# Two chunks to an attention block in a sliding-window attention and SwiGLU kernel

## The chip, the cores and the metric

The kernel runs on one core of a Trainium2 chip. A core has a matrix engine (TensorE, PE in the profile, whose weight loads are listed as PEld), three engines for elementwise work (VectorE or DVE, ScalarE or ACT, GpSimd or POOL), a queue engine (SyncE or SP) and 16 DMA engines that move data between the memory of the chip (DRAM) and the core's working memory (SBUF). Matmul results land in PSUM, a small memory of eight banks. The engines run side by side and meet at semaphores.

The metric is the device time of one execution in microseconds (us). Lower is better.

## The reference

Causal attention with a window of 64 positions, then a feed-forward block with a gate. Cut to what is computed:

```python
B, H, S, D = 8, 8, 576, 64
scores = (1 / sqrt(D)) * q @ k.transpose(0, 1, 3, 2)
rel = pos[:, None] - pos[None, :]
scores = where((rel >= 0) & (rel < 64), scores, -1e9)
attn = softmax(scores)
x = (attn @ v).transpose(0, 2, 1, 3).reshape(4608, 512)
g = x @ w_gate                       # 512 -> 1536
silu = g / (1 + exp(-g))
out = (silu * (x @ w_val)) @ w_out   # 1536 -> 512
```

## The kernel before

**Tiles.** The 4608 tokens are 36 chunks of 128 for attention (`NCH`) and nine groups of 512 for the feed-forward part (`NFC`). A sequence of 576 tokens is nine blocks of 64, so a chunk of 128 may hold the end of one sequence and the start of the next; `var` picks one of three masks for that. A token needs the keys of its own block of 64 and of the block ahead of it only.

**Order.** Every operation is recorded once, in program order, with the buffers that it reads and writes (`_Graph.op`, line 42). `emit` (line 63) gives each engine its operations in that order and puts in the semaphore waits that the buffers ask for. A read after a write on TensorE itself needs no wait; the `after=` of an operation asks for one. At the end SyncE waits for the last transfer of every DMA lane (lines 139 to 142).

**Attention of chunk n.** `load` (line 279) brings q, k and v by GpSimd's DMA queue. `T` (line 321) transposes k and q by DMA on SyncE's queue into `kT` and `qT`. `Sb` (line 350) makes the scores on TensorE, in matmuls that use a quarter of the array (64x64): per pair of heads, the first 64 keys of chunk n against all 128 queries (line 391, 64x128), and, in the lower half of the partitions, the block of 64 ahead of the chunk against the first 64 queries and the chunk's second 64 keys against the second 64 queries (line 395, 64x64 each). ACT takes the exponential into `pt` (line 403), and `Sm` (line 407) multiplies by the mask on DVE. `AVmm` (line 426) multiplies by v, 16 matmuls of 64x65 in each of two phases; phase 1 is recorded with `after=` phase 0. The 65th column is the sum of the exponentials, and `AVn` (line 478) divides by it on DVE (lines 484 and 487). `X` (line 506) transposes the result into `xT` by DMA on SyncE's queue.

`B(n)` (line 496) is one attention block: phase 0 of AV for chunk n, the scores of chunk n+1, phase 1 of AV for chunk n, the division, the mask of chunk n+1.

**Feed-forward of group c.** `F(c, fs)` (line 565) makes one of twelve slices of the hidden layer: four matmuls of 512 columns with `Wg`, four with `Wv` (line 585), a tanh on ACT (line 591) and two products on DVE (lines 593 and 595) into `hT`. `O(c, u)` (line 601) is one output tile of 128 tokens: twelve matmuls of 512 columns (line 611), a copy out of PSUM on ACT (line 616) and a store on ACT's queue (line 618). `O_last` (line 620) makes the last tile in two halves of 256 columns (line 633), evicted by ACT and by DVE.

**The loop.** Groups 0 and 1 are written out by hand, with the first chunks among them. From group 2 on a loop runs (lines 814 to 829): each step u of a group c has the block B(4c+u+4), two F, the output tile O(c-1, u) and one F. So group c's steps carry the attention of group c+1. Blocks end with chunk 35, in group 7; group 8 has none.

**PSUM banks.** `bank` (line 215) hands out four banks in turn to F and O, and four to attention.

Of the kernel before, what the change touches and what calls it, by code (L numbers as in the profile page):

```python
# [4 lines left out]
ACTF = mybir.ActivationFunctionType  # L5
# [16 lines left out]
class _Op:  # L22
    __slots__ = ("i", "eng", "fn", "deps", "dma", "pos", "lane", "occ", "clock", "inc", "count")

    def __init__(self, i, eng, fn, deps, dma):
        self.i, self.eng, self.fn, self.deps, self.dma = i, eng, fn, deps, dma
        self.inc = False
        self.count = 0


class _Graph:
# [31 lines left out]
    def emit(self):  # L63
# [59 lines left out]
        def run(eng, e):  # L123
# [15 lines left out]
            if e == "sp":  # L139
                for lane, o in lanes.items():  # L140
                    k, v = target(o)
                    eng.wait_ge(sem[k], v)
# [9 lines left out]
class _Kernel:  # L152
    NQ = 6
    NV = 10
    NZ = 8
    NP = 4
# [4 lines left out]
    NST = 4  # L161

# [6 lines left out]
    def alloc(self):  # L169
# [10 lines left out]
        self.nmask = sb("nmask", 3 * 128)  # L180
        self.Wg = sb("Wg", NK * DFF)[:, :].rearrange("p (c f) -> p c f", c=NK)
# [31 lines left out]
        self.n_s = 0  # L213

    def bank(self, kind):
# [59 lines left out]
    def init_nmask(self):  # L275
        self.g.op("dve", lambda e: e.tensor_scalar(
            self.nmask[:, :], self.mask[:, :], 1.0, 30000.0, ALU.subtract, ALU.mult), reads=["mask"], writes=["nmask"])

# [78 lines left out]
    def Sa(self, n, bias=False):  # L357
        st = [n, [self.bank("a"), self.bank("a")], False]
        if bias:
            self.Sbias(st)  # L360
        return st
# [15 lines left out]
    def Sb(self, st, mask=True):  # L377
# [23 lines left out]
        for p in range(2):  # L401
            po = pt[:, p::2, :]
            g.op("act", lambda e, po=po, p=p: e.activation(po, sv[p], ACTF.Exp, scale=SCALE), reads=[bx[p][1]], writes=[pk[p]])  # L403
        if not bias and mask:
            self.Sm(n)

    def Sm(self, n):
# [3 lines left out]
        m = self.mask[:, 128 * v:128 * v + 128].unsqueeze(1).to_broadcast([128, H, 128])  # L411
        self.g.op("dve", lambda e: e.tensor_tensor(pt, pt, m, ALU.mult), reads=pk + ["mask"], writes=pk)  # L412
# [5 lines left out]
    def AVa(self, n):  # L418
        bx = [self.bank("a"), self.bank("a")]
# [58 lines left out]
    def AVn(self, st):  # L478
# [9 lines left out]
             reads=bk + [("rc", ir)], writes=[("xb", ix, 0), ("xb", ix, 1)])  # L488

# [6 lines left out]
    def B(self, n):  # L496
# [6 lines left out]
        if n + 1 < NCH:  # L503
            self.Sm(n + 1)

# [28 lines left out]
    def first_T(self, engs):  # L534
        g = self.g
        d = self.ck.rearrange("p j h d -> p h j d")
        self.copy("dve", d, self.fk, [("f", 0), ("f", 1)] + self.fkk, [("ost", 0)])
        for c in range(2):
# [8 lines left out]
            g.op("pe", pe, reads=["ident", ("ost", 0)], writes=[bk])  # L547
# [53 lines left out]
    def O(self, c, u):  # L601
        g = self.g
        ih = c % self.NH
        hT = self.hT[ih]
        io = (4 * c + u) % self.NO
        ost = self.ost[io]
        OB, ok = self.bank("f")

        def pe(e):
            for f in range(NF):  # L610
                r = e.matmul(OB[:, :], hT[:, f, 128 * u:128 * u + 128], self.Wo[:, f, :],  # L611
# [4 lines left out]
        g.op("act", lambda e: e.activation(ost[:, :], OB[:, :], ACTF.Copy), reads=[ok], writes=[("ost", io)])  # L616
        r0 = 512 * c + 128 * u
        g.op("act", lambda e: e.dma_start(self.out[r0:r0 + 128, :], ost[:, :]), reads=[("ost", io)], dma=True)

    def O_last(self, c, u):  # L620
        g = self.g
        ih = c % self.NH
        hT = self.hT[ih]
        ost = self.ost[(4 * c + u) % self.NO]
        io = (4 * c + u) % self.NO
        r0 = 512 * c + 128 * u
        for w, eng in ((0, "act"), (1, "dve")):
            OB, ok = self.bank("f")
            cs = slice(256 * w, 256 * w + 256)

            def pe(e, OB=OB, cs=cs):
                for f in range(NF):
                    r = e.matmul(OB[:, 0:256], hT[:, f, 128 * u:128 * u + 128], self.Wo[:, f, cs],  # L633
                                 start=(f == 0), stop=(f == NF - 1))
                return r

            g.op("pe", pe, reads=self.hTk(ih) + [("Wo", f) for f in range(NF)], writes=[ok])
            d, a = ost[:, cs], OB[:, 0:256]
            if eng == "act":
                g.op("act", lambda e, d=d, a=a: e.activation(d, a, ACTF.Copy), reads=[ok], writes=[("ost", io), ("osth", w)])  # L640
            else:
                g.op("dve", lambda e, d=d, a=a: e.tensor_copy(d, a), reads=[ok, ("ost", io)], writes=[("osth", w)])
            q = "sp" if w == 0 else "act"
            g.op(q, lambda e, d=d, cs=cs: e.dma_start(self.out[r0:r0 + 128, cs], d), reads=[("osth", w)], dma=True)
# [56 lines left out]
    def build(self):  # L701
# [174 lines left out]
```

## Time and profile before

| | us |
|---|---|
| three runs | 335.21, 335.66, 335.78 |
| median | 335.66 |
| the profiled execution: its span | 333.5 |
| TensorE's matmuls, busy | 325.2 |
| DVE, busy | 200.8 |
| ACT, busy | 138.5 |
| GpSimd, busy | 107.1 |
| line 585, 512 columns: 768 matmuls, mean | 0.38 |
| line 611, 512 columns: 420 matmuls, mean | 0.38 |
| line 442, 64x65: 1024 matmuls, mean | 0.20 |
| line 595, one product on DVE | 0.69 |
| line 403, one exponential on ACT | 0.60 |

The profiled execution's own time is not listed apart from its span, from the first to the last instruction. Matmuls are pipelined: a mean of 0.38 us is the time from the start to the modelled end of one, and the next starts long before that end. So times on TensorE are read from start to start. The granted clock of TensorE is full in every slice of the span.

The profile names an engine, the line of the kernel, what is written from what, and the shapes. "Idle before" with an arrow says what an engine waited for; "issue" says that it waited for nothing that the profile shows.

### The profile page before, as it was taken

Reading aid. Unit: us, or ns where it says so; the run is one execution under the profiler, and the core shown is the slowest. Engines: PE = TensorE matmul, PEld = TensorE weight load, DVE = VectorE, ACT = ScalarE, POOL = GpSimd, SP = SyncE. Lnnn points to the kernel's source line nnn. Section 1 sums busy time; section 2 is a strip of 40 time slices with the busy share of each in tenths; the row PEclk is TensorE's granted clock in tenths of the full one; section 3 lists DMA queues with packets and bytes.
Section 4 is the critical chain, followed back from the end, with each engine's and each line's share of the span. In section 5 each row is a group of like instructions: output and inputs, shape, how many; then the busy total and the mean of one; then the engine's idle time right before and its main releaser. Section 6 shows DMA issues by size and latency. Waiting matters only on the chain.

```text
span 333.5 us, 8466 instructions
## 1 busy us (share of the span) xinstructions
PE 325.2 (98%) x3647; PEld 169.7 (51%) x3647; DVE 200.8 (60%) x352; ACT 138.5 (42%) x243; POOL 107.1 (32%) x137
## 2 busy tenths in 40 slices
PE   7899999998999999999999999999999999999996
PEld 7584586655444444444444444444444444444443
DVE  4676884665666666666666656666666666555510
ACT  2646764554444333444444444444444332332311
POOL 8999965644033333333334333500000000000000
PEclk9999999999999999999999999999999999999999
DMA  9999999999999999999999999993343211100012
GB/s 140 180 191 185 178 198 155 187 136 160 174 136 169 118 128 125 129 128 104 130 130 130 116 138 134 108 126 81 79 81 77 74 42 48 47 31 34 31 63 96
DMA packets 157349, 39.36 MB, mean 118 GB/s; under 512 B 144384, under 2 KB 152832, under 8 KB 157312
## 3 DMA queue, kind: packets, MB, share of 16 engines
q0 software_dynamic: 109008, 18.62, 74.2%
q1 hardware_dynamic: 42848, 10.63, 24.0%
q10 hardware_dynamic: 5456, 9.57, 8.5%
q8 instruction: 29, 0.48, 0.6%
q14 instruction: 8, 0.07, 0.1%
HBM read 37.75 MB, written 9.44 MB: 141 GB/s over the span
## 4 chain that ended last, share of the span: by engine, by line
PE 91%; POOL 4%; ACT 1%; issue 1%; DVE 1%; ACTq 0%; POOLq 0%
PE ps L585 56%; PE ps L611 27%; PE ps L442 4%; PE ps L395 1%; PE ps L391 1%; POOL va L295 1%; POOL vs L236 1%; PE ps L344 1%; PE ps L633 1%; POOL Wg L310 1%; PE ps L522 1%; POOL qs L304 1%; POOL Wv L310 0%; DVE uu L593 0%; ACT sig L591 0%
## 5 line engine op out<-in xcount | busy, mean ns | idle before, releaser
L593 DVE SCALAR_TENSOR_TENSOR uu<-sig,ps 128x512 bf16<-128x512 bf16 (+1 forms) x109 | 74.0, 679 | 99.9 <-ACT sig L591 99.8
L585 PE MATMUL ps<-xT,Wg 128*128 128x512 bf16 (+2 forms) x488 | 111.5, 355 | 0.0
L585 PE MATMUL ps<-xT,Wv 128*128 128x512 bf16 (+2 forms) x488 | 111.2, 355 | 0.0
L611 PE MATMUL ps<-Wo,hT 128*128 128x512 bf16 x420 | 96.1, 379 | 1.0 <-issue 1.0
L591 ACT ACTIVATE sig<-ps 128x512 bf16<-128x512 f32 (+1 forms) x109 | 64.7, 593 | 62.8 <-PE ps L585 62.0
L595 DVE SCALAR_TENSOR_TENSOR hT<-uu,ps 128x512 bf16<-128x512 bf16 (+1 forms) x109 | 74.3, 682 | 3.8
L585 PEld LDWEIGHTS ps<-xT,Wv 128*128 128x128 bf16 x488 | 47.1, 98 | 46.4
L611 PEld LDWEIGHTS ps<-Wo,hT 128*128 128x128 bf16 x420 | 40.7, 98 | 50.3 <-issue 1.5
L585 PEld LDWEIGHTS ps<-xT,Wg 128*128 128x128 bf16 x488 | 44.1, 98 | 40.7
L616 ACT ACTIVATE ost<-ps 128x512 f32<-128x512 f32 x35 | 20.9, 597 | 95.1 <-PE ps L611 95.1
L295 POOL DMA_DIRECT2D kn<-in_k_dram x29 | 24.8, 863 | 95.9 <-DMA kT<-kn 95.2
L403 ACT ACTIVATE pt<-ps 128x512 bf16<-128x512 f32 x72 | 39.0, 595 | 20.1 <-PE ps L395 19.3
L295 POOL DMA_DIRECT2D va<-in_v_dram x40 | 35.0, 889 | 0.3 <-issue 0.2
L295 POOL DMA_DIRECT2D qn<-in_q_dram x29 | 25.0, 869 | 10.6 <-DMA qT<-qn 7.6
L487 DVE TENSOR_TENSOR xb<-ps,rc 128x512 bf16<-128x512 f32 x36 | 24.9, 692 | 1.2
L412 DVE TENSOR_TENSOR pt<-pt,mask 128x1024 bf16<-128x1024 bf16 x32 | 21.8, 682 | 5.1 <-ACT pt L403 5.1
L442 PE MATMUL ps<-va,pt 64*64 64x65 bf16 x1024 | 20.7, 197 | 0.6 <-issue 0.4
L442 PEld LDWEIGHTS ps<-va,pt 64*64 64x64 bf16 x1024 | 13.4, 106 | 13.2 <-issue 11.8
L395 PE MATMUL ps<-qT,kT 64*64 64x64 bf16 x576 | 15.3, 193 | 0.0
L391 PE MATMUL ps<-qT,kT 64*64 64x128 bf16 x288 | 14.3, 217 | 0.4 <-ACT qT L234 0.4
L395 PEld LDWEIGHTS ps<-qT,kT 64*64 64x64 bf16 x576 | 11.8, 109 | 0.0
L391 PEld LDWEIGHTS ps<-qT,kT 64*64 64x64 bf16 x288 | 9.2, 106 | 2.8 <-ACT qT L234 1.3
(53 smaller groups left out, 99.6 us busy)
## 6 DMA issues: line engine op xcount, KB each, us to landing
out_dram<-ost ACTq DMA_DIRECT2D x35, 256.0 KB, 2.1
va<-in_v_dram POOLq DMA_DIRECT2D x32, 128.0 KB, 5.8
kn<-in_k_dram POOLq DMA_DIRECT2D x23, 128.0 KB, 4.8
qn<-in_q_dram POOLq DMA_DIRECT2D x23, 128.0 KB, 4.9
Wg<-in_moe_w_gate_dram POOLq DMA_DIRECT2D x6, 256.0 KB, 7.6
Wv<-in_moe_w_val_dram POOLq DMA_DIRECT2D x6, 256.0 KB, 7.6
Wo<-in_moe_w_out_dram POOLq DMA_DIRECT2D x2, 768.0 KB, 14.9
qs<-in_q_dram POOLq DMA_DIRECT2D x3, 256.0 KB, 6.7
```

The costliest lines, as they stand in the source:

```text
L295: self.g.op("pool", lambda e, d=d, a=a: e.dma_start(d, a), writes=ks, dma=True)
L391: e.matmul(sv[p][0:64, c, :], self.kT[ps, c, self.zs(n, 0, 64)], self.qT[ps, c, self.zs(n)], **kw)
L395: r = e.matmul(sv[p][64:128, c, a:a + 64], self.kT[ps, c, ks], self.qT[ps, c, self.zs(n, a, a + 64)], **kw)
L403: g.op("act", lambda e, po=po, p=p: e.activation(po, sv[p], ACTF.Exp, scale=SCALE), reads=[bx[p][1]], writes=[pk[p]])
L412: self.g.op("dve", lambda e: e.tensor_tensor(pt, pt, m, ALU.mult), reads=pk + ["mask"], writes=pk)
L442: x = e.matmul(av[64 * c:64 * c + 64, p, j, :], pt[rows, h, 64 * c:64 * c + 64], vv[rows, h, 0:65], start=first, stop=phase == 1, skip_gro ...
L487: g.op("dve", lambda e: e.tensor_tensor(xo, av[:, :, :, 0:64], rb, ALU.mult), reads=bk + [("rc", ir)], writes=[("xb", ix, 0), ("xb", ix, 1)])
L585: r = e.matmul(bank[:, a * n:a * n + n], W[:, kk, f * 128:f * 128 + 128], xT[:, kk, lo:hi], start=(kk == 0), stop=(kk == NK - 1))
L591: g.op("act", lambda e, G=bank: e.activation(sig[:, 0:w], G[:, 0:w], ACTF.Tanh, scale=0.5), reads=[bk], writes=[("sig", i)])
L593: g.op("dve", lambda e: e.scalar_tensor_tensor(uu[:, 0:w], sig[:, 0:w], 1.0, G[:, 0:w], ALU.add, ALU.mult), reads=[("sig", i), gk], writes ...
L595: g.op("dve", lambda e: e.scalar_tensor_tensor(out, v3(uu), 0.5, v3(V), ALU.mult, ALU.mult), reads=[("uu", i), vk], writes=[("hT", ih, f) ...
L611: r = e.matmul(OB[:, :], hT[:, f, 128 * u:128 * u + 128], self.Wo[:, f, :], start=(f == 0), stop=(f == NF - 1))
```

## The change

It has five parts.

1. From group 3 on (chunk 16), one attention block `B2(n)` serves chunks n and n+1. It stands in the even steps, behind the output tile instead of ahead of the step's first F. Its order is scores of n+2, phase 0 of n, scores of n+3, phase 0 of n+1, phase 1 of n, phase 1 of n+1; then the two masks. The output tile ahead of it is made in two halves (`O2`), the first evicted by ACT, the second by DVE, and its store is issued behind the block. The scores of chunk 17 stand alone in group 2.
2. From chunk 18 (`KW`) scores are made by keys (`Sk`): a chunk's own 128 keys against the queries of their own block of 64 and of the next. AV (`AVk`) then takes the first 64 queries' earlier keys from the `pt` of chunk n-1. The mask is `kmask`, the same for all chunks; what crosses from one sequence to the next is left out of AV.
3. From group 2 on PSUM banks are handed out by the least recent use among all eight (`lru`), attention's in even pairs that are held until read.
4. The rings of loaded and transposed q and k (`NQ`) and of `pt` (`NP`) are longer, and loads and transposes stand elsewhere in the order.
5. At the end SyncE waits only for lanes whose last transfer is a store, in program order.

```diff
@@ emit
             if e == "sp":
-                for lane, o in lanes.items():
-                    k, v = target(o)
-                    eng.wait_ge(sem[k], v)
+                for o in sorted(lanes.values(), key=lambda o: o.i):
+                    if o.out:
+                        k, v = target(o)
+                        eng.wait_ge(sem[k], v)
@@ _Kernel
-    NQ = 6
+    NQ = 8
-    NP = 4
+    NP = 6
+    KW = 18
...
+    def touched(self, j):
+        k = ("ps", j)
+        return max([o.i for o in self.g.readers.get(k, ())] + [o.i for o in self.g.writers.get(k, ())])
+
     def bank(self, kind):
+        if self.lru:
+            j = min((j for j in range(8) if j not in self.held), key=self.touched)
+            return self.ps[j], ("ps", j)
...
+    def pair(self):
+        if not self.lru:
+            return [self.bank("a"), self.bank("a")]
+        ok = [j for j in range(0, 8, 2) if not {j, j + 1} & self.held]
+        j = min(ok, key=lambda j: max(self.touched(j), self.touched(j + 1)))
+        self.held |= {j, j + 1}
+        return [(self.ps[i], ("ps", i)) for i in (j, j + 1)]
...
+    def Sk(self, n):
...
+            for c4 in range(4):
+                for c in range(2):
+                    ks = self.zs(n, 64 * c, 64 * c + 64)
+                    if c == 0:
+                        parts = [(0, 128, self.zs(n))]
+                    elif jz == iz + 1 and not last:
+                        parts = [(0, 128, slice(128 * iz + 64, 128 * iz + 192))]
+                    else:
+                        parts = [(0, 64, self.zs(n, 64, 128)), (64, 128, self.zs(n, 0, 64) if last else self.zs(n + 1, 0, 64))]
+                    for a, b, qs in parts:
+                        for p in range(2):
+                            ps = slice(64 * p, 64 * p + 64)
+                            r = e.matmul(sv[p][64 * c:64 * c + 64, c4, a:b], self.kT[ps, c4, ks], self.qT[ps, c4, qs],
+                                         start=True, stop=True, skip_group_check=True)
...
+    def AVk(self, st, phase):
...
+                    for c in range(2):
+                        if c != r and lone[c]:
+                            continue
+                        rows = slice(64 * r, 64 * r + 64)
+                        back = r == 1 and c == 0
+                        pt, vv = (self.pt[jp], self.va[jv]) if back else (self.pt[ip], self.va[iv])
+                        x0 = 0 if c == r else 64
+                        first = j == 0 and (phase == 0 or (lone[c] and p == 1 - c))
+                        x = e.matmul(av[64 * c:64 * c + 64, p, j, :], pt[rows, h, x0:x0 + 64], vv[rows, h, 0:65],
+                                     start=first, stop=phase == 1, skip_group_check=True)
...
+        done.append(self.g.op("pe", pe, reads=rd, writes=[b[1] for b in bx], after=done[0] if phase else None))
...
+    def B2(self, n):
+        ss = [m for m in (n + 2, n + 3) if m < NCH]
+        st = []
+        for i in range(2):
+            if i < len(ss):
+                self.Sx(ss[i])
+            st.append(self.AVa(n + i))
+            self.AVp(st[i], 0)
+        for a in st:
+            self.AVp(a, 1)
+            self.AVn(a)
+        for m in ss:
+            self.Sm(m)
...
+    def O2(self, c, u):
+        io = (4 * c + u) % self.NO
+        self.Omm(c, u, 0, 256, "act", [("osth", io)])
+        self.Omm(c, u, 256, 512, "dve", [("ost", io)])
@@ build
         self.B(10)
+        self.load(16, "kq")
...
         self.B(11)
+        self.load(17, "kq")
...
-        for c in range(2, NFC):
+        self.lru = True
+        self.init_kmask()
+        for u in range(4):
+            n = 12 + u
+            for m in ((18,), (19, 20), (21,), (22,))[u]:
+                self.load(m, "kq")
+            self.load(n + 2, "v")
+            self.B(n)
+            X(n)
+            for m in ((15, 16), (17,), (18,), (19,))[u]:
+                self.Tkq(m)
+            if u == 3:
+                self.T(20, "q")
+            F(2, (3 * u,))
+            F(2, (3 * u + 1,))
+            O(1, u)
+            if u == 3:
+                self.Sx(17)
+                self.Sm(17)
+            F(2, (3 * u + 2,))
+        for c in range(3, NFC):
             for u in range(4):
                 n = 4 * c + u + 4
-                if n < NCH:
-                    self.load(n + 4, "kq")
-                    self.load(n + 2, "v")
-                    self.B(n)
-                    self.X(n)
-                    self.Tkq(n + 3)
                 F(c, (3 * u,))
                 F(c, (3 * u + 1,))
-                if n < NCH or u < 3:
+                two = n < NCH and u % 2 == 0
+                if two:
+                    self.O2(c - 1, u)
+                elif n < NCH or u < 3:
                     O(c - 1, u)
+                if two:
+                    self.B2(n)
+                    self.store(c - 1, u)
+                    X(n)
+                    X(n + 1)
+                    for m in (n + 4, n + 5):
+                        self.T(m, "k")
+                    for m in (n + 5, n + 6):
+                        self.T(m, "q")
+                    for m in (n + 7, n + 8):
+                        self.load(m, "kq")
+                    for m in (n + 2, n + 3):
+                        self.load(m, "v")
                 F(c, (3 * u + 2,))
```

`Sx(n)` is `Sk(n)` from chunk 18 and `Sb(n)` without its mask before; `AVp` is `AVk` from chunk 18 and `AVmm` before. `Omm` is the body of `O` for a range of columns, and `store` is its store.

More of the change, by code (lines that the diff above doesn't have):

```diff
@@ L357, in Sa @@
     def Sa(self, n, bias=False):
[L358 removed]
+        st = [n, self.pair(), False]
         if bias:
@@ L418, in AVa @@
     def AVa(self, n):
-        bx = [self.bank("a"), self.bank("a")]
+        bx = self.pair()
         j = bx[0][1][1]
@@ L601, in O, with Omm @@
     def O(self, c, u):
-        g = self.g
-        ih = c % self.NH
-        hT = self.hT[ih]
         io = (4 * c + u) % self.NO
[L606 to L611, printed above, removed]
-                             start=(f == 0), stop=(f == NF - 1))
-            return r
-        g.op("pe", pe, reads=self.hTk(ih) + [("Wo", f) for f in range(NF)], writes=[ok])
[L616 to L620, printed above, removed]
+        self.Omm(c, u, 0, 512, "act", [("ost", io), ("osth", io)])
+        self.store(c, u)
+    def O2(self, c, u):
+        io = (4 * c + u) % self.NO
+        self.Omm(c, u, 0, 256, "act", [("osth", io)])
+        self.Omm(c, u, 256, 512, "dve", [("ost", io)])
+    def Omm(self, c, u, lo, hi, eng, wr):
         g = self.g
```

96 lines of the change are left out of this document (75 added, 21 removed).

## The prediction

> **What bounds the kernel now.** I read the page first: busy time, slices, the chain that ended last.
>
> ```profile
> PE 325.2 (98%) x3647; PEld 169.7 (51%) x3647; DVE 200.8 (60%) x352; ACT 138.5 (42%) x243; POOL 107.1 (32%) x137
> PE   7899999998999999999999999999999999999996
> DMA  9999999999999999999999999993343211100012
> PE 91%; POOL 4%; ACT 1%; issue 1%; DVE 1%; ACTq 0%; POOLq 0%
> ```
>
> TensorE (PE) is busy in every slice and makes 91% of the chain; no other engine passes 60%. So only what shortens TensorE's own sequence, or what lies after its last matmul, moves the end. Next, the timeline of TensorE alone around the attention block of one chunk in the steady part (start, duration, line, count):
>
> ```profile
> 202.38 1.03 PE L585 MATMUL ps<-xT,Wv 128*128 128x512 bf16 x4
> 203.34 0.32 PE L442 MATMUL ps<-va,pt 64*64 64x65 bf16 x16
> 203.49 0.22 PE L391 MATMUL ps<-qT,kT 64*64 64x128 bf16 x2
> 203.55 0.22 PE L391 MATMUL ps<-qT,kT 64*64 64x128 bf16 x2
> 203.60 0.22 PE L391 MATMUL ps<-qT,kT 64*64 64x128 bf16 x2
> 203.66 0.22 PE L391 MATMUL ps<-qT,kT 64*64 64x128 bf16 x2
> 203.74 0.32 PE L442 MATMUL ps<-va,pt 64*64 64x65 bf16 x16
> 203.99 1.04 PE L585 MATMUL ps<-xT,Wg 128*128 128x512 bf16 x4
> ```
>
> Durations overlap, so starts are to be read. The Wg group ahead starts at 201.52, so four 512-wide matmuls take 0.86 us and the Wv group's slot ends at 203.24. The block therefore costs 203.99 - 203.24 = 0.75: 0.10 to go from whole-array to quarter-array matmuls, 0.15 first AV half, 0.25 scores, 0.15 second AV half, 0.10 to go back. Other rows of the same view, without and with neighbours:
>
> ```profile
> 280.13 0.72 PE L442 MATMUL ps<-va,pt 64*64 64x65 bf16 x32
> 280.78 1.04 PE L585 MATMUL ps<-xT,Wg 128*128 128x512 bf16 x4
> ...
> 32.16 0.24 PE L391 MATMUL ps<-qT,kT 64*64 64x128 bf16 x2
> 32.53 0.82 PE L585 MATMUL ps<-xT,Wg 128*128 128x512 bf16 x3
> ...
> 118.39 0.32 PE L442 MATMUL ps<-va,pt 64*64 64x65 bf16 x16
> 118.69 0.59 PE L585 MATMUL ps<-xT,Wg 128*128 128x512 bf16 x2
> ```
>
> At 280.13, the last chunk, both AV halves stand alone: 0.65 where 0.15 + 0.15 + 0.10 = 0.40 would do. The second half waits for a semaphore of the first (the `after=` in AVmm), so its start cannot come before 0.40 after the first's start, which is what scores between them fill exactly (203.34 to 203.74). At 118.69 a new group c begins behind a block: 0.30 instead of 0.25.
>
> The timeline of all engines at the end, then the closing waits by their line:
>
> ```profile
> 327.41 2.78 PE L633 MATMUL ps<-Wo,hT 128*128 128x256 bf16 x24
> 329.33 0.36 SPq L644 DMA_DIRECT2D out_dram<-ost  x1
> 330.23 0.42 DVE L642 COPY ost<-ps 128x256 f32<-128x256 f32 x1 [11.80 <-PE ps L633]
> 330.69 0.34 ACTq L644 DMA_DIRECT2D out_dram<-ost  x1
> ...
> L142 SPq EVENT_SEMAPHORE  x20: 17/28/28, 329.7 to 332.8; - x20
> ```
>
> The last store, issued at 330.69, lands after the page's 1.7 us: 332.40. SyncE's wait for that lane is not the last: lanes are waited in order of first use, and the last of the 20 waits starts at 332.77.
>
> **The parts and their costs.** Sums are against the profiled execution, span 333.5; the median of the runs, 335.66, lies 2.2 above it, and I carry the difference over.
>
> 1. *Paired blocks.* Before, chunks 16 to 35 (groups 3 to 7) have 20 blocks: 19 x 0.75 + (0.10 + 0.65) = 15.0. After, the order in a pair is scores n+2, AV first half n, scores n+3, first half n+1, second half n, second half n+1. The last one waits as at 280.13: its start is 0.40 after the first half n+1 started, with only one half (0.15) between. That is an added stall of 0.40 - 0.30 = 0.10, given back out of the 0.20 that the spared switch is worth; behind it on TensorE stands F(c,3u+2), which moves with it. Scores by keys are 16 matmuls, all of L391's form. That form is spaced 0.056 on its quarter: 4 x 0.056 = 0.22 at the low end, Sb's 0.25 (0.27 just after a switch: 32.53 - 32.16 - 0.10) at the high end. All Sk matmuls of a whole step are of the L391 row, so I take 0.24 for the first, 0.23 for the second. A pair: 0.10 + 0.24 + 0.15 + 0.23 + 0.40 + 0.15 + 0.10 = 1.37, nine times 12.33. The last pair has no scores: AV starts at 0, 0.15, 0.40, 0.55, end 0.70, with both switches 0.90. Sx(17) becomes a block of its own: 0.10 + 0.37 = 0.47. Sum 13.70, so **-1.3** (-1.5 with 0.22 each; -0.8 with 0.27 and 0.25).
>
> 2. *Semaphores inside the block.* Sk's second call waits for four semaphores, AV's for two or three. At 118.69 additional waits behind an AV half cost 0.05; at 203.49, with a shorter list, nothing. Between 0 and 0.10 a pair; I take 0.02, nearer to the row inside a block: **+0.2** (0 to +0.9). The first half n+1 takes the bank of the second output half, so it waits for DVE's copy: L642's row starts 2.82 after L633's first start and lasts 0.42, ready 0.62 after the tile's slot (24 x 0.109 = 2.62) ends. The first half n+1 comes 0.10 + 0.24 + 0.15 + 0.23 = 0.72 after it. Cover 0.10; if gone, each late 0.1 us costs 0.9 in all.
>
> 3. *Halved output tiles.* 24 matmuls at 0.109 against 12 at 0.216: 2.62 for 2.59, ten times: **+0.3**. Each moves half an eviction to DVE, 0.42 of it; DVE is busy 21.4 of 34 us in the window 194 to 228, so this is hidden, as are three small kmask copies. By the Trainium skill's page TensorEngine Tiling (Array Packing), section Instruction Overhead, each matmul carries about 60 cycles of overhead, at the 2.4 GHz of its page Trainium Kernel Development and Optimization (NeuronCore Architecture) 25 ns; 12 more matmuls would be an estimated 0.3 us a tile, 3 us in all, and the sum would turn to +1.3. The row of L633 disagrees: 0.109 for half the columns.
>
> 4. *Starts of groups.* F(c,0) now follows F(c-1,11), not a block. 118.69 shows 0.05; five such starts, **-0.2** (0 to -0.3). The waits then lie behind long matmuls, as at F(8,0), which starts on its slot.
>
> 5. *Moves off TensorE.* The same 78 transposes and 125 loads are issued. SyncE's queue gets six in a row: X(n), X(n+1), four T. The first is ready when DVE has normalised n, some 2.1 us into the block; six issues of 1.19 to 1.27 bring the last to 8.5, landing 3.9 later at 12.4, needed at the next pair, 17.0 later (two steps of 8.52: blocks at 203.34 and 211.86). X(n+1) goes out at 3.3, lands at 8.1, and F(c+1,0) at the earliest comes 1.27 + 4 x 1.73 + 2.59 = 10.8 into it. POOL may run two chunks further ahead (NQ 8). ACT's store of the halved tile moves behind four exps; its buffer is needed four tiles later. DVE has 2 x 0.89 + 2 x 0.68 = 3.1 us of block work ahead of the next F; LRU over eight banks gives F(3u+2) banks whose exps (0.54 each) end before, and the others come round over 5 us later. All 0; the lack of cover is priced in the rivals.
>
> 6. *Closing waits.* Only lanes with stores, the last store's last: 332.77 - 332.40: **-0.4**.
>
> Sum -1.3 + 0.2 + 0.3 - 0.2 - 0.4 = **-1.4: 334.3 us**.
>
> **The rivals.**
>
> *A. An early stall goes too.* Between 16 and 92 us three idles end by "issue": 0.33, 0.42 and this one:
>
> ```profile
> 80.54 1.47 PE L611 MATMUL ps<-Wo,hT 128*128 128x512 bf16 x6 [1.00 <-issue]
> ```
>
> Nothing is waited for by semaphore; the instruction queue's 29 packets in 0.48 MB on a loaded DMA (174 GB/s over 16 to 92 us) are the suspect. NQ = 8 lets loads 16 and on start without waiting from about 55 us, and their order changes. The stall may vanish: -1.2 more (six matmuls in 1.30 take 2.47), 333.1. It may as well grow by as much: 335.5.
>
> *B. The gain is eaten.* A second late wait in each pair (0.10 as in 2) takes 0.9, and scores as slow as Sb another 0.5: 334.3 + 1.4 = 335.7, no change.
>
> *C. Slower: instruction supply.* All three idles stand at or just behind dense small matmuls. A pair issues 96 matmuls and as many weight loads in 1.3 us, a block before 56 and 56 in 0.75. If a refill came late in every pair, each mean 0.58 (1.75 / 3) would cost 10 x 0.58 = 5.8: 340.1; from three stalls on, the gain is gone. Against it: the 24 blocks after 80 us show no such idle, and DMA moves 49 to 126 GB/s there from 126 us on. The Trainium skill's page Runtime: NRT & Kernel Launch, section Instruction fetch mechanics, has refills in blocks of 256 instructions, mostly hidden by the pace of issue; 0.48 MB in 29 packets agrees with that size, and the three idles agree with "mostly".
>
> *D. Slower: SyncE's queue.* If each of six issues took 2.2 (the largest of L515 and L328) and the landing 10.5 (the largest), the last would land 23.6 into a period of 17, 6.6 us late: 340.9 for one such pair. It decides once queue and landing take over 14.9 from X(n)'s issue. The medians, 1.27 and 3.9, speak against it.
>
> **How the numbers follow.** This kernel's runs can't tell under 0.2% (0.67 us) from no change. Forecast 0.60 (334.3; its own range 333.7 to 334.9 by the ends of 1 to 4), A less 0.11, A more or B 0.16, C 0.06, D 0.03, other faults 0.04. Faster: 0.60 + 0.11, and a little of B, 0.73; same 0.15; slower 0.12. Range 332.7 to 335.7: it takes in A on both sides and B to its centre, and leaves out some 0.17.
>
> **What would show it.** Right: one run of 64x64 matmuls every 17 us that costs about 1.37, with the last AV half 0.40 behind the start of its first half; L633's spacing in the new tiles; SyncE's last wait right behind the last store. Wrong: idle of TensorE ahead of AV n+1 (DVE's copy late), ahead of Sk (transposes), "issue" inside pairs, or the stretch up to 92 us longer.

## The result, and the profile after

| | us |
|---|---|
| before, four runs beside it | 335.72 (335.21 to 336.22) |
| changed kernel, four runs | 333.94 (333.57 to 335.11) |
| ratio, 95% interval | 0.9956 [0.9935, 0.9977] |
| predicted | 334.3 (332.7 to 335.7) |

The changed kernel is faster by 0.4%. Its profiled execution is the longest of the four: 335.11, span 333.1. This page says that nothing has changed sides: TensorE still bounds the kernel, and the loads of q and k take longer to land (11.3 and 10.8 us; the page of the kernel before has 4.8 for k).

```profile
PE 324.1 (97%) x3615; PEld 181.7 (55%) x3615; DVE 207.2 (62%) x365; ACT 134.4 (40%) x243; POOL 107.0 (32%) x137
...
PE   7899999998999999999999999999999999999996
...
PE 92%; POOL 2%; DMA 2%; issue 1%; ACT 1%; DVE 1%; POOLq 0%
...
kn<-in_k_dram POOLq DMA_DIRECT2D x23, 128.0 KB, 11.3
qn<-in_q_dram POOLq DMA_DIRECT2D x23, 128.0 KB, 10.8
```

The timeline of TensorE around one pair (193.46 to 194.87), and around the last one, which has no scores (start, duration, line, count). A wide window merges AV halves that touch, so the rows from 193.55 to 194.61 come from narrow ones:

```profile
193.55 0.42 PE L468 MATMUL ps<-qT,kT 64*64 64x128 bf16 x16
193.80 0.30 PE L498 MATMUL ps<-va,pt 64*64 64x65 bf16 x16
193.97 0.42 PE L468 MATMUL ps<-qT,kT 64*64 64x128 bf16 x16
194.19 0.32 PE L498 MATMUL ps<-va,pt 64*64 64x65 bf16 x16
...
194.61 0.32 PE L498 MATMUL ps<-va,pt 64*64 64x65 bf16 x16
194.87 1.04 PE L702 MATMUL ps<-xT,Wg 128*128 128x512 bf16 x4
...
278.52 0.88 PE L498 MATMUL ps<-va,pt 64*64 64x65 bf16 x64
279.33 1.04 PE L702 MATMUL ps<-xT,Wg 128*128 128x512 bf16 x4
```

Read from start to start, with the 0.09 that lie ahead of the first matmul: 0.09 + 0.25 + 0.17 + 0.22 + 0.42 + 0.26 = 1.41 for one pair. The 0.42 from the first half of n+1 to the second half of n+1 holds 32 matmuls in 0.26 and a wait of 0.16. The last pair costs 0.81 + 0.09 = 0.90, as forecast.

At the start of group 3 there is an idle that the kernel before does not have. Its SyncE and TensorE timelines there (the bracket is idle before, and what ended it):

```profile
112.25 1.19 SPq L632 DMA_TRANSPOSE xT<-xb  x1
...
117.99 1.03 PE L702 MATMUL ps<-xT,Wv 128*128 128x512 bf16 x4
119.40 1.02 PE L702 MATMUL ps<-xT,Wg 128*128 128x512 bf16 x4 [0.39 <-issue]
```

The DMA view of 110.9 to 112.4 us (kind, count, us from issue to landing):

```profile
xT<-xb SPq DMA_TRANSPOSE x1, 7.1
```

Group 2's last slice ends its slot at 118.85; group 3 starts at 119.40. The page calls the idle "issue", but the landing beside it says what was missing: chunk 15's transposes, issued at 112.25, landed 7.1 later, at 119.3. The end, from the timeline:

```profile
329.60 0.36 SPq L757 DMA_DIRECT2D out_dram<-ost  x1
330.50 0.42 DVE L257 COPY ost<-ps 128x256 f32<-128x256 f32 x1 [11.81 <-PE ps L738]
330.96 0.34 ACTq L757 DMA_DIRECT2D out_dram<-ost  x1
```

SyncE's closing waits by their line (count, ns of one, first and last start):

```profile
L144 SPq EVENT_SEMAPHORE  x4: 28/28/28, 330.0 to 332.7; - x4
```

Four waits instead of 20, the last starts at 332.7, right behind the last store's landing.

Summed over the trace against the profiled execution of the kernel before (span 333.52), with a second profiled execution of the changed kernel (x0 below, span 332.23) beside it:

| us | predicted | on record | x0 |
|---|---|---|---|
| blocks of chunks 16 to 35 with waits and group starts (steps 1, 2, 4): 15.11 before; 14.11, 13.99 after | -1.3 | -1.00 | -1.12 |
| ten halved tiles, 24 x 0.109 for 12 x 0.216 | +0.3 | +0.24 | +0.24 |
| idle ahead of F(3,0) | 0 | +0.55 | +0.47 |
| first matmul, and idles up to 92 us | 0 | +0.47 | -0.25 |
| from the last matmul's start to the end: 3.60 before; 2.96, 2.95 after | -0.4 | -0.64 | -0.65 |
| sum | -1.4 | -0.38 | -1.31 |
| span | | -0.37 | -1.29 |

The fourth row differs between two executions of one program: the first feed-forward matmul stands at 17.32 and 16.60 (16.59 before), the idle at 79 us takes 1.43 and 1.14 (1.17 before). x0's profiled execution is its kernel's median one, the one on record the longest of four; x0 is the better one to read.

### The profile page after: what moved, and what is told of

Its sections match the earlier page's. It is cut to its first block, busy times and chain, and to the rows that moved or that the text cites. A ratio compares the mean times of both kernels' runs of the same rounds, so it can differ in the third digit from the quotient of the medians.

```text
span 333.1 us, 8426 instructions
## 1 busy us (share of the span) xinstructions
PE 324.1 (97%) x3615; PEld 181.7 (55%) x3615; DVE 207.2 (62%) x365; ACT 134.4 (40%) x243; POOL 107.0 (32%) x137
## 4 chain that ended last, share of the span: by engine, by line
PE 92%; POOL 2%; DMA 2%; issue 1%; ACT 1%; DVE 1%; POOLq 0%
PE ps L702 56%; PE ps L738 28%; DMA va<-in_v_dram 2%; PE ps L498 2%; PE ps L535 2%; PE ps L468 2%; POOL vs L257 1%; PE ps L372 1%; PE ps L423 1%; PE ps L419 1%; PE ps L639 1%; POOL qs L332 1%; ACT kT L255 0%; ACT qT L255 0%; POOL ks L332 0%
## 5 line engine op out<-in xcount | busy, mean ns | idle before, releaser
L738 PE MATMUL ps<-Wo,hT 128*128 128x256 bf16 (+1 forms) x564 | 99.0, 329 | 1.3 <-issue 1.3
L738 PEld LDWEIGHTS ps<-Wo,hT 128*128 128x128 bf16 x564 | 54.9, 98 | 41.7 <-issue 1.8
L702 PEld LDWEIGHTS ps<-xT,Wg 128*128 128x128 bf16 x488 | 44.8, 98 | 42.8 <-issue 0.8
L255 ACT ACTIVATE ost<-ps 128x512 f32<-128x512 f32 (+1 forms) x36 | 19.2, 532 | 83.3 <-PE ps L738 83.3
L323 POOL DMA_DIRECT2D qn<-in_q_dram x29 | 25.0, 872 | 10.9 <-DMA va<-in_v_dram 3.5
L477 ACT ACTIVATE pt<-ps 128x512 bf16<-128x512 f32 x36 | 18.6, 602 | 11.6 <-PE ps L468 11.6
L431 ACT ACTIVATE pt<-ps 128x512 bf16<-128x512 f32 x36 | 19.4, 595 | 9.2 <-PE ps L423 8.8
L257 DVE COPY ost<-ps 128x256 f32<-128x256 f32 x11 | 4.7, 425 | 26.2 <-PE ps L738 26.2
L445 DVE TENSOR_TENSOR pt<-pt,mask 128x1024 bf16<-128x1024 bf16 x14 | 9.6, 684 | 8.6 <-ACT pt L431 8.6
L577 DVE RECIPROCAL rc<-ps 128x8 f32<-128x8 f32 x36 | 7.3, 203 | 7.6 <-PE ps L498 5.6
L445 DVE TENSOR_TENSOR pt<-pt,kmask 128x1024 bf16<-128x1024 bf16 x18 | 11.5, 683 | 0.0
L535 PE MATMUL ps<-va,pt 64*64 64x65 bf16 x448 | 8.9, 196 | 0.6 <-issue 0.5
L498 PE MATMUL ps<-va,pt 64*64 64x65 bf16 x544 | 9.1, 194 | 0.0
## 6 DMA issues: line engine op xcount, KB each, us to landing
kn<-in_k_dram POOLq DMA_DIRECT2D x23, 128.0 KB, 11.3
qn<-in_q_dram POOLq DMA_DIRECT2D x23, 128.0 KB, 10.8
```

The source lines that it names most:

```text
L255: self.g.op("act", lambda e: e.activation(d, a, ACTF.Copy), reads=reads, writes=writes)
L323: self.g.op("pool", lambda e, d=d, a=a: e.dma_start(d, a), writes=ks, dma=True)
L498: x = e.matmul(av[64 * c:64 * c + 64, p, j, :], pt[rows, h, x0:x0 + 64], vv[rows, h, 0:65], start=first, stop=phase == 1, skip_group_check ...
L702: r = e.matmul(bank[:, a * n:a * n + n], W[:, kk, f * 128:f * 128 + 128], xT[:, kk, lo:hi], start=(kk == 0), stop=(kk == NK - 1))
L738: r = e.matmul(OB[:, 0:n], hT[:, f, 128 * u:128 * u + 128], self.Wo[:, f, lo:hi], start=(f == 0), stop=(f == NF - 1))
```

## The experiments

In each the diff is against the changed kernel unless said otherwise, and the ratio is to the kernel before in the same batch (its medians were 335.36, 335.39, 335.15 and 335.20). In the traces of x1, x2, x3, x6 and x11 the first matmul behind each block has no record; its start is taken as 0.226 ahead of the second's, which is the spacing in the other traces.

### The end alone, and single blocks

x1: the kernel before, with the closing waits of the change and nothing else.

```diff
-                for lane, o in lanes.items():
-                    k, v = target(o)
-                    eng.wait_ge(sem[k], v)
+                for o in sorted(lanes.values(), key=lambda o: o.i):
+                    if o.out:
+                        k, v = target(o)
+                        eng.wait_ge(sem[k], v)
```

> The kernel before with one part of the change alone: SyncE's closing waits on stores only. Theory (the gain is mode switches spared plus 0.4 at the end): 0.35 to 0.45 us less than before, and in the trace the last store's wait is followed at once by the end. The profile of the changed kernel has a closing stretch, from the last matmul's start to the span's end, that is 0.65 shorter than before (2.96 against 3.60), of which 0.36 are the waits and 0.29 lie in GpSimd's part of the closing barrier. Rival: those 0.29 belong to the change too, then 0.65 less. Second rival: the whole gain is the end, then 1.5 less.

Measured: 335.00, ratio 0.9989 [0.9977, 1.0001]. The interval alone leaves it open; the trace shows the step: from the last matmul's start to the end 3.25 where the kernel before has 3.60, -0.35.

x6: the changed kernel's banks, rings and closing waits, but single blocks with scores by queries and whole output tiles.

```diff
-    KW = 18
+    KW = 36
...
+                if n < NCH:
...
+                    self.load(n + 2, "v")
+                    self.B(n)
+                    self.X(n)
+                    self.Tkq(n + 3)
...
-                    self.B2(n)
```

> The changed kernel with parts 1 and 2 undone from group 2 on: one block per chunk ahead of the step, whole output tiles, scores by queries; least-recently-used banks, longer rings, earlier loads 16 and 17 and the closing waits stay. Theory: each chunk's block costs 0.74 again and the output tiles 0.3 less in all, so this kernel stands only the end's 0.4 below before, 335.3, and about 1.1 above the changed kernel. Rival (banks and rings carry the gain): at or below the changed kernel's 333.9.

Measured: 334.73, ratio 0.9983 [0.9971, 0.9995]: 0.63 below the kernel before in the same batch, nearer to the theory than to the rival. A block away from a group's start costs 0.742, as before, and the twenty cost 15.14 (15.11 before). So the banks by least recent use and the longer rings change nothing in a block; what x6 gains lies at the end (2.94 from the last matmul's start, 3.60 before). The change's gain in the blocks goes with what x6 takes out together: the pairing, the scores by keys and the halved tiles.

### Inside the pair

x2: the output tile ahead of the pair is whole, and ACT evicts it.

```diff
-                    self.O2(c - 1, u)
+                    self.Omm(c - 1, u, 0, 512, "act", [("ost", io), ("osth", io)])
```

> The changed kernel with a whole output tile ahead of each pair (twelve matmuls of 512 columns, evicted by ACT alone). Theory by rows: ACT's copy starts 0.31 behind the last matmul's start and takes 0.60, ready 0.69 behind the slot's end; the first AV half n+1, which takes that bank's pair, comes 0.73 behind it, so no wait over 0.05; the exponentials start 0.13 later, F's bank is still free in time; the tile itself is 0.03 shorter, ten times: 0.3 less than the changed kernel, 333.6. Rival (the halves hide a real wait): TensorE waits 0.1 to 0.3 in each pair, 0.7 to 2.4 more, 334.6 to 336.3.

Measured: 334.48, ratio 0.9983 [0.9967, 0.9998]; a pair takes 1.50. The theory's price missed, and the wait that the rival expected is there. One pair on TensorE and ACT's copy, from the timeline:

```profile
191.96 0.42 PE L468 MATMUL ps<-qT,kT 64*64 64x128 bf16 x16
192.21 0.29 PE L498 MATMUL ps<-va,pt 64*64 64x65 bf16 x16
192.40 0.42 PE L468 MATMUL ps<-qT,kT 64*64 64x128 bf16 x16
192.72 0.72 PE L498 MATMUL ps<-va,pt 64*64 64x65 bf16 x48
...
192.06 0.60 ACT L255 ACTIVATE ost<-ps 128x512 f32<-128x512 f32 x1 [2.86 <-PE ps L738]
```

From its view of waits between 124 and 282 us (engine, what waited, for what; us, times, longest):

```profile
PEld ps L498 <- ACT ost L255: 0.2, 1, 0.2
```

From the second scores to the first half of n+1 it takes 0.32 (0.22 in the changed kernel): that half takes the output tile's bank, and ACT's copy of the whole tile ends at 192.66. The view lists only idles over 0.15 us, so it names this wait once; in the trace the half's first weight load starts 0.05 behind the end of that copy in all nine pairs. The halved tile costs 0.024 and makes a pair 1.40 to 1.41 where the whole one makes it 1.50: it pays for itself, which the prediction, pricing it by its matmuls alone, did not see.

x4: all scores by queries, and with them AV and masks as before (`AVmm`).

```diff
-    KW = 18
+    KW = 36
```

> The changed kernel with scores by queries in all chunks (KW = 36): 24 score matmuls a chunk with the three masks, instead of 16 with one. Theory: the first scores of a pair cost 0.27 and the second 0.25, against 0.25 and 0.22 measured, so 0.05 a pair, 0.4 to 0.5 in all, 334.4. Rival: the wait for the second half of the last chunk or for DVE's copy takes up the difference, no change.

Measured: 334.99, ratio 0.9997 [0.9983, 1.0011]: of the gain nothing is left. A pair takes 1.535, all blocks 15.15 for 13.99, 1.16 more where some 0.05 a pair were forecast. The timeline of x4, cut to the rows that start a phase:

```profile
192.66 0.24 PE L419 MATMUL ps<-qT,kT 64*64 64x128 bf16 x2
...
192.91 0.19 PE L535 MATMUL ps<-va,pt 64*64 64x65 bf16 x1
...
193.18 0.24 PE L419 MATMUL ps<-qT,kT 64*64 64x128 bf16 x2
...
193.40 0.19 PE L535 MATMUL ps<-va,pt 64*64 64x65 bf16 x1
...
194.10 1.04 PE L702 MATMUL ps<-xT,Wg 128*128 128x512 bf16 x4
```

From start to start here and in x0's pair at 192.66: first scores 0.247 and 0.248; first half of n 0.275 and 0.172; second scores 0.221 and 0.220; first half of n+1 to second half of n+1 0.446 and 0.424; the last half 0.25 in both. So the theory put the cost in the wrong place: an AV half starts as soon behind 24 score matmuls as behind 16. Of the 0.126 that the pair is longer, 0.10 lie between the first half of n and the second scores: that half's starts spread over 0.13 instead of 0.10 us, and the gap behind them is 0.14 instead of 0.07. What ends this gap the trace does not say. In x4 the nine pairs cost more than 18 single blocks would (13.78 against 18 x 0.742 = 13.36): paired blocks with scores by queries gain nothing.

x3: another order of the same phases, so that no AV half stands right behind its own first half.

```diff
         for i in range(2):
-            if i < len(ss):
-                self.Sx(ss[i])
             st.append(self.AVa(n + i))
             self.AVp(st[i], 0)
+            if i < len(ss):
+                self.Sx(ss[i])
```

> The changed kernel with each AV first half ahead of the scores in the pair: first half n, scores n+2, first half n+1, scores n+3, second halves. Theory: the last second half then has scores and a second half between itself and its first half (0.22 + 0.13, over the 0.27 of the semaphore), so its wait of 0.12 to 0.15 goes; a pair costs 1.25 instead of 1.37 to 1.47, nine pairs make 1.1 to 1.5 less than the changed kernel, about 332.7. The second scores take the bank that DVE empties and come 0.64 behind the tile's slot, ready at 0.62, so no new wait over 0.05. Rival (the gap is matmul issue, not the semaphore): a pair stays at 1.4 and the time is that of the changed kernel, 333.9.

Measured: 333.26, ratio 0.9941 [0.9922, 0.9959]; a pair takes 1.34, all blocks 13.56. One pair on TensorE:

```profile
191.52 0.32 PE L498 MATMUL ps<-va,pt 64*64 64x65 bf16 x16
191.66 0.40 PE L468 MATMUL ps<-qT,kT 64*64 64x128 bf16 x16
191.89 0.30 PE L498 MATMUL ps<-va,pt 64*64 64x65 bf16 x16
192.10 0.42 PE L468 MATMUL ps<-qT,kT 64*64 64x128 bf16 x16
192.35 0.42 PE L498 MATMUL ps<-va,pt 64*64 64x65 bf16 x32
```

The result lies between the theory (1.25) and the rival (1.4). Both second halves now run without a gap between them, so the wait of 0.16 is gone. Only 0.07 of it is gained: from the first half of n+1 to the second scores it takes 0.21, 0.11 of it a gap that ends with DVE's copy of the output tile (191.62 to 192.05), which now stands ahead of the scores instead of ahead of an AV half. Another 0.05 is lost behind the last half, in the wait that x7 shows next.

x7: a second half between the two scores.

```diff
+        x = [self.AVa(n)]
+        self.AVp(x[0], 0)
+        if ss:
+            self.Sx(ss[0])
+        x.append(self.AVa(n + 1))
+        self.AVp(x[1], 0)
+        self.AVp(x[0], 1)
+        self.AVn(x[0])
+        if len(ss) > 1:
+            self.Sx(ss[1])
+        self.AVp(x[1], 1)
+        self.AVn(x[1])
```

> The changed kernel with the pair in another order: first half n, scores n+2, first half n+1, second half n, scores n+3, second half n+1. Theory (two waits make the pair cost 1.41 instead of 1.24: a second half too close behind its first half, and the bank of the second output half asked for too early): each second half now has 0.35 of other work since its first half, over the 0.27 to 0.30 that the semaphore takes, and the last pair of banks is first used 0.76 behind the tile's slot, after the 0.68 that the order with first halves first has shown; a pair costs 1.24 to 1.28, 1.2 to 1.6 less in all than the changed kernel, 0.6 to 0.9 less than the earlier order. Rival: what is left in a pair is dispatch of the semaphore instructions, then 1.34 as in the earlier order.

Measured: 334.01, ratio 0.9959 [0.9944, 0.9974]; a pair takes 1.342, as in x3. That is the rival's number, but the trace shows another cause than dispatch. Gaps of 0.04 and 0.06 remain ahead of the first half of n+1 and of the second scores, and then F waits behind the pair. ACT's first exponential of scores n+2 and TensorE's last half and F, and from the view of waits between 124 and 282 us:

```profile
194.78 0.60 ACT L477 ACTIVATE pt<-ps 128x512 bf16<-128x512 f32 x1 [1.42 <-PE ps L468]
...
195.08 0.32 PE L498 MATMUL ps<-va,pt 64*64 64x65 bf16 x16
195.43 1.04 PE L706 MATMUL ps<-xT,Wg 128*128 128x512 bf16 x4
...
PEld ps L706 <- ACT pt L477: 0.6, 3, 0.2
```

From the last half to F it takes 0.35, and 0.26 in the changed kernel: F takes the bank that this exponential reads, and starts 0.05 behind its end (195.38). So it is in all nine pairs of x3, x7, x8 and x9, and in none of the changed kernel, where the scores of n+2 stand first and their exponential ends 0.13 earlier in the pair. Without this wait x7's pair would take an estimated 1.25 by these rows, inside the theory's 1.24 to 1.28.

The median does not show the shorter pairs. The profiled execution, the longest of the seven (335.38), idles 1.87 us at the start of group 3; whether the others do no trace shows:

```profile
117.48 1.03 PE L706 MATMUL ps<-xT,Wv 128*128 128x512 bf16 x4
120.21 1.02 PE L706 MATMUL ps<-xT,Wg 128*128 128x512 bf16 x4 [1.71 <-DVE uu L714]
```

### Chunk 17, and the idle at the start of group 3

x0: the changed kernel once more, for a second profile.

> The changed kernel again, on the chip and in the rounds of the next three. Its profile on record has a 0.55 stall at 118.6 ahead of F(3,0), a start 0.72 later than the kernel before and a 1.43 idle at 79.4. Theory: these differ from run to run; the stall at 118.6 is a late landing of X(15) and is mostly absent, the pairs cost 1.37 to 1.47 again, the span is near 332.0 and the time 333.9. Rival: the stall belongs to the change and is there again, the time is the same but pairs cost less.

Measured: 334.21, ratio 0.9959 [0.9942, 0.9977]. The idle ahead of F(3,0) is there again, 0.47, against the theory, and the pairs take 1.35 to 1.51, mean 1.40. They differ mostly in the gap ahead of the second scores, 0.02 to 0.15; what sets it is open.

x8 is x7, x9 is x3 and x10 is the changed kernel, each with the scores of chunk 17 moved into the block of chunk 15:

```diff
-            self.B(n)
+            self.B(n, extra=17 if u == 3 else None)
...
-            if u == 3:
-                self.Sx(17)
-                self.Sm(17)
```

> As the interleaved kernel, and the scores of chunk 17 stand in the block of chunk 15 instead of in one of their own. Theory: a block of its own costs 0.47, in a block the scores cost about 0.25; 0.2 less than the interleaved kernel, too little for the times to tell, but seen in the trace as one block of about 1.0 in place of 0.74 and 0.47. Rival: the added scores push the exponentials and X(15) back and F(3,0) waits for it, 0.1 to 0.5 more.

> Phase order AV first half n, scores n+2, AV first half n+1, scores n+3, both second halves (x3_phase_order), and the scores of chunk 17 inside the block of chunk 15 instead of standing alone. Theory: both gains are of separate places and add up: the own block of chunk 17 costs 0.47 and its 24 matmuls in a block that is there anyway cost 0.25, so 0.22 below the 333.26 of the phase order alone: 333.0. The idle at 118 was not in the run of the phase order, so nothing is gained there. Rival: what x8 gained over x7 (0.96) is mostly the scores of 17, by their place and not by the idle: then 332.4. No gain, 333.3, if the second scores in the block wait for banks.

> The changed kernel, with the scores of chunk 17 inside the block of chunk 15 and nothing else. Theory: the own block (0.47) goes and 0.25 comes; the chunk's exponentials and mask no longer stand between O(1,3) and the start of group 3. The idle at 118 is a landing of chunk 15's transposes, which this leaves where it is: 0.2 below the changed kernel, 334.0 against before's 335.4. Rival: the idle at 118 hangs on the work around the own block, and goes with it, as in x8_interleaved_s17: 0.2 + 0.5 below, 333.5.

Measured: x8 333.05, ratio 0.9939 [0.9927, 0.9950]; x9 333.46, 0.9942 [0.9920, 0.9964]; x10 334.02, 0.9959 [0.9943, 0.9975]. x10's median is where the theory put it, but its ratio is that of the changed kernel, and x9's that of x3: the 0.2 was not gained. x8's median is 0.96 below x7's, but their intervals overlap, and the block gives none of it. The own block cost 0.47, and in all three the block of 15 grows from 0.74 to 1.235, by 0.49. Timeline of TensorE and DVE in x10:

```profile
110.28 0.32 PE L535 MATMUL ps<-va,pt 64*64 64x65 bf16 x16
110.65 0.24 PE L419 MATMUL ps<-qT,kT 64*64 64x128 bf16 x2
...
111.03 1.04 PE L706 MATMUL ps<-xT,Wg 128*128 128x512 bf16 x4
...
109.91 0.69 DVE L714 SCALAR_TENSOR_TENSOR uu<-sig,ps 128x512 bf16<-128x512 bf16 x1 [3.04 <-ACT sig L712]
```

The AV half's last matmul starts at 110.41, the scores at 110.65. DVE reads the bank that they take until 110.60, and the view of waits of x10 names it, first here and then between 112 and 120 us:

```profile
PEld ps L419 <- DVE uu L714: 0.2, 1, 0.2
...
PEld ps L706 <- DMA xT<-xb: 1.0, 1, 1.0
```

The spared switches turned into a wait for a bank, as part of the gain did in x3 and x7.

The second of these lines is the idle at the start of group 3, which x10 still has. Here the profile names what ends it, chunk 15's transposes, and the timeline of TensorE does too:

```profile
119.43 1.04 PE L706 MATMUL ps<-xT,Wg 128*128 128x512 bf16 x4 [0.46 <-DMA xT<-xb]
```

So the rival, that the idle hangs on the own block, fell too: x10 has the idle without that block, and x8 and x9 had landings of 5.0 and under 6.6 us in their profiled executions.

x5: rings of six, as before.

```diff
-    NQ = 8
+    NQ = 6
```

> The changed kernel with rings of six (as before) instead of eight for loaded and transposed q and k; nothing else. Theory: the longer ring lets GpSimd start loads earlier, the DMA engines are fuller while the first groups run, and so the last transposes of chunk 15, issued at about 112, land 7 us later, which is the idle of TensorE ahead of F(3,0) at 118. With six, that idle (0.55 and 0.47 in the two profiled runs of the changed kernel) is gone, and the median falls by about that: 333.7, against 334.2 for the changed kernel beside the same runs of before (335.4). Rival: the idle comes from where the transposes of chunk 15 stand in the order, which the ring does not change: idle again, 334.0 to 334.3. Second rival: a ring of six makes later loads wait, and transposes come late for a pair: over 334.5, with idle ahead of scores.

Measured: 334.41, ratio 0.9979 [0.9960, 0.9997]. The loads' landings fall to 6.1 and 6.3, as the theory said, and the idle stays, 1.01: the theory fell. A shorter ring does not give shorter pairs either (blocks 14.09).

x11: rings of eight, but q and k of chunks 20 to 22 loaded a step later.

```diff
-            for m in ((18,), (19, 20), (21,), (22,))[u]:
+            for m in ((18,), (19,), (20,), (21,))[u]:
...
+                if n == 16:
+                    self.load(22, "kq")
                 F(c, (3 * u,))
```

> The changed kernel with the q and k of chunks 20, 21 and 22 loaded one step (8.5 us) later in GpSimd's queue; rings of eight as in the change; TensorE's and SyncE's orders are as there. x5_short_ring showed that the length of the ring does not cause the idle ahead of F(3,0) at 118. Theory: it comes from the loads of group 3, which the change puts a chunk further ahead: they are in flight when the transposes of chunk 15 are issued (12 to 15 transfers on their way at 112), so these land 7 to 8 us after their issue, with room for 6.6. With a chunk less in flight they land in under 6.6, TensorE does not wait at 118, the loads' medians fall below 9 us (11.3 and 10.8 in the changed kernel), and the median is 0.3 to 0.5 lower: 333.6 where before has 335.3. Rival: the landing of that one transfer varies by itself (4.8 to 8.4 in the profiled kernels so far, with and without idle): idle or none, loads' medians as they were, and a median within 0.2 of 334.1. Second rival: the load of 22 comes too late for the first pair: idle ahead of its scores at 125, over 334.4.

Measured: 333.62, ratio 0.9957 [0.9942, 0.9972], loads landing in 9.7 and 9.8. The median is the theory's and the idle is absent, but the ratio is that of the changed kernel (0.9956, 0.9959), the loads' landings did not fall below 9, and the runs spread as x0's do (333.0 to 335.0; x0 333.0 to 335.4). This doesn't settle it.

What the profiles together show. Eleven kernels have the same order around the start of group 3, but for chunk 17's scores in x8 to x10; the transposes of chunk 15 have 6.6 us there. From issue to landing, by the DMA view or the wait of TensorE that it ended:

| landing, us | idle ahead of F(3,0) |
|---|---|
| x8 5.0, x4 5.5, x2 5.8, x11 5.9, x3 6.3, x9 under 6.6 | none |
| x0 7.0, changed kernel 7.1, x10 7.2, x5 7.5, x7 8.4 | 0.47, 0.55, 0.63, 1.01, 1.87 |

The kernel before had 6.9 and a landing of 5.6. That a late landing makes the idle is shown; why it is late in some executions is open. It needs neither the ring of eight (x5) nor the own block of chunk 17 (x10). Among the kernels with rings of eight the three longest idles go with the three slowest medians of k's loads (11.3, 13.6 and 15.9, where the others have 8.6 to 10.9), which speaks for a fuller DMA in those executions and proves no cause.

## Why the prediction was right, and where it was off

The mechanism held for the kernel as changed: with one switch to quarter-array matmuls and back for two chunks the blocks fall to 13.99, and x6, without the pairing, its scores by keys and its halved tiles, keeps 15.14. But the pairing does not gain by itself: x4, which has it with scores by queries, has 15.15. In x0 the 1.12 are 0.75 in nine pairs (0.08 each, of the 0.20 at which the spared switch was priced), 0.58 in the last pair and 0.26 at the starts of groups, less 0.47 for chunk 17's own block. By the steps:

1. *Paired blocks*, -1.3 with steps 2 and 4: -1.00 and -1.12. A pair was put at 1.37, with semaphores at 1.39; the means over nine are 1.41 and 1.40. The last pair is right at 0.90, chunk 17's block at 0.47. Of the miss of 0.18 in x0, half is the pairs; the other half is the kernel before, whose block takes 0.742 and not 0.75: 0.16 less to gain, 0.06 of it made up for by step 4. (With 0.22 for both scores the step's own sum comes to -1.6, not -1.5.)
2. *Semaphores inside the block*, +0.2: in x0's pair at 192.66 the first half of n takes 0.172 until the second scores start, for the 0.15 taken, 0.07 of it a gap; the wait between the AV halves makes 0.424 from start to start, for 0.40. Together 0.05 in this pair, inside the bounds given (0 to 0.10) and above the 0.02 chosen; the rest of the pair was 0.01 under its price. The cover over DVE's copy held in the changed kernel. x2 shows the price without cover, there over ACT's copy: 0.10 a pair, as the step's "0.9 in all" had it.
3. *Halved tiles*, +0.3: +0.24, as priced. The 60 cycles for each matmul of the Trainium skill's page TensorEngine Tiling (Array Packing), section Instruction Overhead, do not appear: 24 matmuls take 2.62 where by the page they would take an estimated 2.9.
4. *Starts of groups*, -0.2: in the kernel before, the five blocks at such starts cost 0.26 more than 0.742 each, and that is gone.
5. *Moves off TensorE*, all 0: failed at one place. "The last lands before the next pair" was argued for the pairs of groups 3 to 7; the start of group 3, where chunk 15's transposes have 6.6 us, was not priced. It cost 0.47 and 0.55 in the two profiles. The landings of loads doubled, which has no price seen on TensorE.
6. *Closing waits*, -0.4: x1 alone shows -0.35, as worked out. The change has 0.29 more at the end, in GpSimd's closing barrier (0.37 from its start to its end before, 0.08 after), and every kernel built from the changed one has it, x6 too, while x1 has not. It was not foreseen, and why is open.

So the sum was near (x0 -1.31 for -1.4) in part by luck: a lost 0.2 in the blocks and 0.5 of idle were met by 0.25 more at the end, unforeseen, and by an early stretch 0.25 shorter by chance.

The rivals: A, the early stall, came in both directions: the idle at 79 us takes 1.43 and 1.14 in two executions of the changed kernel, and 0.80 to 1.99 over the profiled kernels. So chance is enough for it; that the change has no part in it is not shown. B, a second late wait of 0.10 in each pair, is what x2 shows, with 1.50 a pair; the halves keep it away. C, instruction supply, fell: no pair of the changed kernel has a gap over 0.2. D, SyncE's queue, fell for the pairs; its kind of mishap, a transposed chunk landing late, came at another place and at a tenth of the price.

The experiments point to faster orders: x8, x3 and x9 stand at 0.9939, 0.9941 and 0.9942 against before, the changed kernel at 0.9956 and 0.9959. Their blocks are 0.4 shorter in the trace (13.99 in x0; 13.56 in x3; 13.57 and 13.61 in x8 and x9, the 0.49 for chunk 17 included). The intervals overlap with the changed kernel's and with each other's; none is shown to be the best.

## What to carry to other kernels

When phases are merged to save switches, count the waits that the spared work was covering: a fixed latency between two phases of the same result, and the eviction of whatever bank the next phase takes. Each new order moved part of the wait to another place (x3 to DVE's copy, x3 and x7 to ACT's exponential ahead of F) before it made it smaller, so ask of each order what the next phase's bank is waiting for. Merging alone gained nothing here (x4); it paid together with shorter scores and halved tiles. A cheap edit that looks like a cost (two half tiles for one) can be what keeps a bank free in time. Price every step that moves on the first and last round of a loop by itself, where its cover is shortest, and take a second profile before a difference of 0.5 us is explained.

## What the runs showed of the hardware

- The matmuls behind a set of scores start after the same time whether the set has 16 matmuls of 64x128 (x0) or 24 of 64x128 and 64x64 (x4): 0.248 and 0.247 us right behind a change of tile size, 0.220 and 0.221 in the second place. x4's pair is longer in the phase ahead of its second scores (0.275 for 0.172), cause open.
- One transposing transfer of the same size at the same place took 5.0 to 8.4 us from issue to landing over eleven profiled kernels.
- An idle that the profile calls "issue" can be a DMA's: the same idle was called "issue" in the changed kernel, "DVE" in x7 and "DMA xT" in x10, and in each the landing of the transposes falls at its end.
